# Quad 0's keys in two pieces: a third as floats over SyncE with a cast on ScalarE, and the packed queries in two transfers

## The chip, the cores and the metric

The kernel runs on one core of a Trainium2 chip. The metric is the device time of one execution in microseconds (us), as the median of several runs. A measurement of this kernel tells a difference from no change at about 0.2%, which is 0.49 us here.

## The reference

Eight batches of eight heads attend twice, and a two-layer block with a squared ReLU follows. The first attention has 32 packed queries `p` per head over 576 keys and values; the second has the 576 queries `q` over the 32 packed rows that the first one made.

```python
def _attn_ref(q, k, v, p):                     # q, k, v: 8 x 8 x 576 x 64, p: 8 x 8 x 32 x 64
    def sm_attn(qq, kk, vv):
        s = scale * np.matmul(qq, kk.transpose(0, 1, 3, 2))
        s = s - np.max(s, axis=-1, keepdims=True)
        a = np.exp(s)
        a = a / (np.sum(a, axis=-1, keepdims=True) + 1e-09)
        return np.matmul(a, vv)
    p_packed = sm_attn(p, k, v)
    return sm_attn(q, p_packed, p_packed)
def _moe_ref(x, w_in, w_out):                  # 4608 x 512, 512 x 2048, 2048 x 512
    h = x @ w_in
    r = np.maximum(h, 0.0)
    return (r * r) @ w_out
```

All inputs and the output are float32 in device memory.

## The kernel before

Heads are taken in quads: four heads of 32 rows fill the 128 partitions, so that each of the eight batches (0 to 7) has two quads, 0 and 1. Matmul operands are bf16; the accumulators in PSUM are float32.

The order of the work is written out by hand in the string `ORDER` (L50). `run` takes it word by word, and each word issues the instructions of one step, so that the order on every engine, and on the queues that DMAs are issued from, is the order of the words. The first letters name the step, and the digits name batch and quad (or batch, half and block). A suffix `:a`, `:v` or `:p` picks ScalarE (ACT), VectorE (DVE) or GpSimd (POOL). The words that matter at the head are these.

- `pf` (`p_first`, L222) loads the packed queries of batches 0 and 1 as floats into a part of `gT` that is not yet in use (`p_f`). It issues three DMAs from SyncE (SP), at L225, L268 and L270. A quad whose rows are turned needs two transfers, which `load_rows` makes (L268, L270).
- `P0` and `P1` (`p_cast`, L231 and L235) scale and cast the packed queries of batch 0 and of batch 1 on DVE and turn them there in 32x32 blocks.
- `Lk00`, `Lk01`, `Lv00`, `Lv01` (`load1`) load keys and values of quads 0 and 1 of batch 0. `LA0` and `LB0` load the queries, `Wi..` and `Wo.` the weights. All of these are issued by POOL and cast from float32 to bf16 on the way, and they go through one queue in this order.
- `kT00`, `kT01` (`st_k`, L351) transpose the keys of a quad on DVE, 128x576 pairs each.
- `Z18.0`, `Z2.0`, `Z7.0` and so on (`busy`, L335) are matmuls on zeros, 128x512 each, that keep PE busy; their number is fixed in the word. They start after a memset of the zeros (L187).
- `s100`, `s101` (L375) are the 24 score matmuls of a quad, `m100`, `m101` (L401) the row maxima on DVE, `x100`, `x101` (L413) the exponentials on ACT, and `eT..` (L433), `eo..` (L421) the transposes of the result on PE and their copies to SBUF.

After the first attention of batch 0 come `pv0`, `pp0` (the packed rows), then the second attention in two parts (`A` with 256 columns, `B` with 320), and from about 21 us on the words of the two-layer block: `h` (first layer, L590), `r` (ReLU, L595 or L597), `q` (square, L635 or L633) and `o` (second layer, L648). They are mixed with the attention of the next batch.

The order begins so (L51):

```
pf Lk00 Lk01 Lv00 Lv01 I P0 LA0 P1 Wi00 kT00 Wi10 LB0 Z18.0 s100 Wi01 kT01 Wi11 m100 Z2.0 s101 x100 m101 Wi21 x101 Z7.0
```

Of the kernel before, what the change touches and what calls it, by code (L numbers as in the profile page):

```python
# [9 lines left out]
ALU = mybir.AluOpType  # L10
# [11 lines left out]
D = 64  # L22
# [12 lines left out]

WIDE = range(2, 8)
# [14 lines left out]
pf Lk00 Lk01 Lv00 Lv01 I P0 LA0 P1 Wi00 kT00 Wi10 LB0 Z18.0 s100 Wi01 kT01 Wi11 m100 Z2.0 s101 x100 m101 Wi21 x101 Z7.0  # L51
eT00 eo00:v Z1.0 eT01 rd0 eo01:v Wi20 Z2.0 pv0 pp0 qA01 Lk10 Z2.0 pt0 bd0 qA00 po0:a Z2.1 zA0 Lk11 tA00 tA01 mA01 mA00
sA01:v xA01 sA00:v uA01 xA00 qB00 Wo0 qB01 aA01:p uA00 Z18.1 zB0 wa00 Lv11 tB00 tB01 aA00:p Wa00:a mB00 Z2.1 wa01 mB01
sB00:p Wa01:a TA01 Z1.1 wb01 TA00 Lv10 wb00 xB00 sB01:v h0.0.8 h0.0.9 Wb01:a Wb00:v h0.0.1 h0.0.0 xB01 uB00 r0.0.8:a
r0.0.1:a h0.0.2 uB01 r0.0.9:a aB00:p r0.0.0:a h0.0.3 r0.0.2:v q0.0.4:a h0.0.11 Wo2 aB01:v h0.0.10 q0.0.0:a TB00 TB01
r0.0.3:a r0.0.10:v r0.0.11:a h0.1.0 h0.1.1 q0.0.1:v q0.0.5:a h0.1.9 r0.1.0:v h0.1.8 r0.1.1:a r0.1.9:v LA1 w100 w101
q0.1.0:v r0.1.8:a h0.1.10 W100:v W101:a h0.1.11 h0.1.3 q0.1.4:p h0.1.2 r0.1.10:a r0.1.3:v r0.1.11:a h0.0.4 kT10 r0.1.2:a
LB1 h0.0.13 r0.0.4:a h0.0.5 q0.1.1:a h0.1.14 r0.0.13:v q0.1.5:p h0.0.14 r0.0.5:v h0.1.13 r0.1.14:a kT11 h0.0.15
r0.0.14:a h0.0.6 q0.0.2:a h0.0.12 Wo1 r0.0.15:v s11 r0.1.13:a r0.0.12:v r0.0.6:a Wo3 h0.1.15 q0.0.7:v q0.0.6:a h0.0.7
r0.1.15:v h0.1.4 r0.0.7:a Lv20 h0.1.6 m110 r0.1.4:a h0.1.5 r0.1.6:a h0.1.7 m111 h0.1.12 q0.0.3:a o2.0 x110 r0.1.5:v o2.1  # L60
r0.1.12:v q0.1.7:p o0.0 x111 o3.0 r0.1.7:a eT10 q0.1.6:a o0.1 Pr q0.1.2:v eT11 q0.1.3:v eo10:a o1.0 rd1 eo11:v o3.1 pv1
o1.1 pp1 o0.2 pt1 o1.2 bd1 po1:a o3.2 qA11 w011 w111 qA10 W011:a o0.3 W111:v o2.2 Lv21 o1.3 qB10 zA1 qB11 w010 o2.3 tA11
W010:a tA10 o3.3 mA11 zB1 mA10 sA11 w110 o0.4 sA10 tB11 W110:a o2.4 tB10 o1.4 mB11 xA11 o0.5 xA10 mB10 o1.5 uA10 o2.5
Lk20 sB11 o0.6 uA11 o0.7 xB11 aA10 o1.6 c0:a aA11 o1.7 sB10 o3.4 TA10 c1:a d0 TA11 o2.6 uB11 xB10 h1.0.1 Lk21 h1.0.6 Px
o2.7 r1.0.1:v d1 r1.0.6:v o3.5 aB11 h1.0.0 c2:a h1.0.2 Pt o3.6 r1.0.0:a TB11 o3.7 r1.0.2:a d2 Lk31 Pu:v q1.0.0:a h1.0.4
h1.0.3 c3:a o4.0 r1.0.3:v r1.0.4:a o5.0 kT20 q1.0.1:a h1.0.7 d3 h1.0.5 uB10 o5.1 r1.0.5:a o4.1 r1.0.7:v q1.0.2:a aB10
h1.0.10 h1.0.8 q1.0.3:v r1.0.10:a o4.2 kT21 Lq2 h1.0.9 r1.0.8:a o5.2 r1.0.9:a h1.0.12 TB10 s12 q1.0.4:v r1.0.12:a
h1.0.14 m120 o5.3 Lv30 r1.0.14:a h1.1.1 m121 h1.1.3 r1.1.1:a o5.4 x120 r1.1.3:v h1.0.11 o4.3 r1.0.11:v x121 h1.1.7 kT31
h1.0.15 eT20 Lq3 q1.0.5:a o4.4 r1.0.15:v eT21 r1.1.7:v q1.0.7:a o5.5 rd2 eo20:v eo21:a h1.0.13 h1.1.2 r1.0.13:v o4.5
r1.1.2:v q1.0.6:a h1.1.6 pv2 r1.1.6:v h1.1.8 pp2 h1.1.0 q1.1.1:a r1.1.8:v Lk30 o5.6 qT21 q1.1.3:a o4.6 h1.1.12 r1.1.0:a  # L70
bd2 pt2 qT20 o4.7 bs2:a Lk40 h1.1.5 po2:v r1.1.12:a o5.7 q1.1.0:v c4:a h1.1.10 r1.1.5:v c5:a s22 d4 r1.1.10:v h1.1.4
o6.0 t221 r1.1.4:a h1.1.9 d5 o7.0 q1.1.2:a t220 h1.1.13 r1.1.9:a o6.1 qT30 r1.1.13:a Lq4 h1.1.11 q1.1.4:a m221 w120 w121
r1.1.11:a o6.2 m220 W121:a h1.1.14 h1.1.15 W120:v Lv31 o6.3 r1.1.14:a q1.1.6:a o7.1 o6.4 sb21:v r1.1.15:a Lv40 o7.2
q1.1.5:a kT30 o7.3 q1.1.7:a o7.4 sb20:v Lk41 x221 o6.5 qT31 o7.5 x220 o6.6 su21 o6.7 o7.6 su20 c6:a o7.7 w020 a221 c7:a
d6 w021 o8.0 W020:a a220 o8.1 d7 o8.2 aT21 W021:a o8.3 aT20 o8.4 Lq5 h2.0.1 h2.0.0 r2.0.1:v o8.5 r2.0.0:a o8.6 q2.0.0
h2.0.2 h2.0.3 r2.0.2:v o9.0 Lk50 o8.7 r2.0.3:v h2.0.5 c8:a s13 q2.0.1 r2.0.5:a h2.0.4 d8 m130 o10.0 r2.0.4:a h2.0.6 kT40
h2.0.7 r2.0.6:a o10.1 r2.0.7:a q2.0.2 h2.0.10 Lk51 x130 m131 o9.1 h2.0.8 r2.0.10:a q2.0.3 o9.2 r2.0.8:a kT41 h2.0.13
x131 eT30 h2.0.9 r2.0.13:v o10.2 eo30:a rd3 r2.0.9:v h2.1.1 eT31 q2.0.4 h2.0.14 r2.1.1:a o10.3 r2.0.14:v eo31:a h2.0.11
Lk61 o9.3 r2.0.11:v o9.4 h2.0.12 h2.1.5 q2.0.5 r2.0.12:a pv3 r2.1.5:v h2.0.15 q2.0.6 h2.1.4 pp3 r2.0.15:a o9.5 r2.1.4:v
# [55 lines left out]
class Kernel:  # L135
# [128 lines left out]
    def load_rows(self, x, s, n=0, engine=None):  # L264
# [558 lines left out]
```

## Time and profile before

| what | value |
|---|---|
| three runs | 243.16, 243.31, 243.33 us, median 243.31 us |
| the profiled execution | 243.35 us, of which the span from the first to the last instruction is 241.5 us |
| granted TensorE clock, mean | 0.999 |
| PE busy | 235.4 us (97% of the span) |
| DVE busy | 203.0 us (84%) |
| ACT busy | 142.0 us (59%) |
| POOL busy | 74.8 us (31%) |
| DMA queue of POOL (q0) | 18.55 MB, 54.2% of 16 engines |
| DMA queue of SP (q1) | 9.51 MB, 14.8% of 16 engines |

The profiled execution stands within 0.04 us of the median, so that differences worked out inside it can be set against the runs. Outside the span lie 1.85 us. The page's 40 slices show PE at nine tenths or more nearly everywhere, with the zeros counted as work.

### The profile page before, as it was taken

How to read it: one execution, taken by the hardware profiler on the slowest of the kernel's cores; microseconds unless marked ns; L12 is line 12 of the kernel's file. 1: busy time of each engine (PE TensorE's matmuls, PEld its weight loads, DVE VectorE, ACT ScalarE, POOL GpSimd, SP SyncE). 2: the span in 40 equal slices, each digit the busy share in tenths (PEclk: the TensorE clock that was granted, in tenths of full speed). 3: DMA queues.
4: the chain of work that ended last, by engine and by line, in shares of the span. 5: the costliest groups of instructions: out<-in, count | busy, mean ns of one | idle time of the engine just before them, and what ended most of it. 6: DMA issues, size and time to landing. Idle time of an engine off the chain costs nothing.

```text
span 241.5 us, 6098 instructions
## 1 busy us (share of the span) xinstructions
PE 235.4 (97%) x2415; PEld 125.9 (52%) x2415; DVE 203.0 (84%) x459; ACT 142.0 (59%) x308; POOL 74.8 (31%) x123
## 2 busy tenths in 40 slices
PE   8998899999999999999999999999999999999994
PEld 3544564456544564456555554465545644555542
DVE  2679986999998889989998889997899879987740
ACT  2216993697897557955693647774495346733300
POOL 8637783594585262044303340002000000000000
PEclk9999999999999999999999999999999999999999
DMA  6999999999999979259932974217113111111224
GB/s 103 189 199 210 202 206 206 181 209 210 194 169 212 236 103 136 51 71 209 107 86 28 206 107 66 62 34 105 37 24 76 46 46 43 43 46 43 50 61 109
DMA packets 33404, 28.51 MB, mean 118 GB/s; under 512 B 8160, under 2 KB 28384, under 8 KB 33376
## 3 DMA queue, kind: packets, MB, share of 16 engines
q0 software_dynamic: 26848, 18.55, 54.2%
q1 hardware_dynamic: 6384, 9.51, 14.8%
q8 instruction: 19, 0.31, 0.5%
q14 instruction: 9, 0.07, 0.1%
q10 hardware_dynamic: 144, 0.07, 0.1%
HBM read 37.22 MB, written 9.44 MB: 193 GB/s over the span
## 4 chain that ended last, share of the span: by engine, by line
PE 91%; DMA 4%; ACT 2%; DVE 1%; SPq 0%; issue 0%; POOL 0%; POOLq 0%
PE ps_o L648 50%; PE ps_h L590 26%; PE ps_wp L574 4%; PE ps_idle L335 3%; PE ps_s L375 3%; DMA k_b<-in_k_dram 2%; PE ps_e1T L433 2%; PE ps_pv L457 1%; DMA out_dram<-o_sb 1%; ACT r L595 1%; ACT wp L419 1%; SPq L679 0%; PE ps_ppT L496 0%; ACT gT L633 0%; DVE kT L351 0%
## 5 line engine op out<-in xcount | busy, mean ns | idle before, releaser
L648 PE MATMUL ps_o<-w_out_bf,gT 128*128 128x512 bf16 (+1 forms) x576 | 147.3, 378 | 0.0
L590 PE MATMUL ps_h<-a2T,wp 128*128 128x288 bf16 (+2 forms) x512 | 89.9, 286 | 1.3 <-DVE rs L543 0.6
L595 ACT ACTIVATE r<-ps_h 128x288 bf16<-128x288 f32 (+2 forms) x159 | 61.0, 415 | 47.2 <-PE ps_h L590 42.5
L648 PEld LDWEIGHTS <-gT 128*128 128x128 bf16 x576 | 54.4, 98 | 43.1 <-issue 3.4
L590 PEld LDWEIGHTS <-wp 128*128 128x128 bf16 x512 | 47.7, 98 | 42.4 <-issue 8.0
L597 DVE TENSOR_SCALAR r<-ps_h 128x288 bf16<-128x288 f32 (+2 forms) x97 | 41.9, 447 | 11.1 <-PE ps_h L590 10.5
L635 DVE TENSOR_TENSOR gT<-r 128x576 bf16<-128x576 bf16 (+2 forms) x104 | 45.1, 446 | 2.8 <-ACT r L595 1.8
L419 ACT CAST wp<-ps_wp 128x1024 bf16<-128x1024 f32 (+1 forms) x29 | 27.7, 974 | 9.0 <-PE ps_wp L574 8.9
L419 ACT COPY o_sb<-ps_o 128x512 f32<-128x512 f32 x26 | 15.2, 589 | 12.3 <-PE ps_o L648 10.1
L268 POOL DMA_DIRECT2D k_b<-in_k_dram x28 | 15.2, 544 | 16.5 <-DVE kT L351 7.3
L268 POOL DMA_DIRECT2D q_b<-in_q_dram x16 | 11.0, 690 | 28.8 <-DVE qT L363 25.4
L313 POOL DMA_DIRECT2D v_b<-in_v_dram x12 | 9.4, 779 | 31.5 <-PE ps_pv L457 30.5
L335 PE MATMUL ps_idle<-gT 128*128 128x512 bf16 (+1 forms) x59 | 16.1, 417 | 1.2 <-DVE gT L187 1.2
L413 ACT ACTIVATE e<-ps_s,nm 128x576 bf16<-128x576 f32 x16 | 11.8, 742 | 7.5 <-DVE nm L401 7.4
L633 ACT ACTIVATE gT<-r 128x512 bf16<-128x512 bf16 (+1 forms) x21 | 14.0, 690 | 0.5 <-DVE r L597 0.3
L535 ACT ACTIVATE e<-d 128x576 f32<-128x576 f32 (+2 forms) x20 | 11.7, 599 | 4.1 <-DVE d L529 3.9
L351 DVE STREAM_TRANSPOSE kT<-k_b 128x576 uint32<-128x576 uint32 x16 | 12.3, 767 | 0.6 <-DMA k_b<-in_k_dram 0.6
L363 DVE STREAM_TRANSPOSE qT<-q_b 128x576 uint32<-128x576 uint32 (+2 forms) x20 | 12.4, 633 | 0.0
L541 DVE TENSOR_REDUCE sums<-e 128x18 f32<-128x576 f32 (+2 forms) x20 | 12.2, 608 | 0.1
L401 DVE TENSOR_REDUCE nm<-ps_s 128x1 f32<-128x576 f32 x16 | 11.5, 739 | 0.8 <-PE ps_s L375 0.7
L523 DVE TENSOR_REDUCE mx<-s 128x18 f32<-128x576 f32 (+2 forms) x20 | 11.6, 609 | 0.0
L529 DVE TENSOR_TENSOR d<-s,mx 128x576 f32<-128x576 f32 (+2 forms) x19 | 11.6, 631 | 0.0
(60 smaller groups left out, 179.3 us busy)
## 6 DMA issues: line engine op xcount, KB each, us to landing
out_dram<-o_sb SPq DMA_DIRECT2D x65, 128.0 KB, 2.9
v_b<-in_v_dram POOLq DMA_DIRECT2D x12, 256.0 KB, 5.5
w_out_bf<-in_moe_w_out_dram POOLq DMA_DIRECT2D x4, 512.0 KB, 12.4
q_b<-in_q_dram POOLq DMA_DIRECT2D x6, 288.0 KB, 5.3
q_b<-in_q_dram POOLq DMA_DIRECT2D x12, 144.0 KB, 5.7
k_b<-in_k_dram POOLq DMA_DIRECT2D x12, 108.0 KB, 4.1
gT<-in_v_dram POOLq DMA_DIRECT2D x4, 288.0 KB, 9.7
w_in_bf<-in_moe_w_in_dram POOLq DMA_DIRECT2D x4, 256.0 KB, 9.8
```

Of the source, the lines that this page charges most:

```text
L268: engine.dma_start(x[n:], s[:P - n])
L335: self.nc.tensor.matmul(ps[:, :m], lhsT=self.nought[:, :P], rhs=self.nought[:, :m], start=True, stop=True)
L351: self.nc.vector.transpose(t["kT"][:].rearrange("p s e -> p (s e)").bitcast(U32), t["k"][:].rearrange("p t d -> p (t d)").bitcast(U32))
L363: self.nc.vector.transpose(out.bitcast(U32), x.bitcast(U32))
L419: engine.copy(out, x)
L541: nc.vector.reduce_sum(out=sums[:, x], in_=t["e2"][:, x], axis=AX.X)
L590: self.nc.tensor.matmul(ps, lhsT=t["wp"][:, fb // n, fb % n * P:(fb % n + 1) * P], rhs=t["a2T"][:, s0:s1], start=(qd == 0), stop=(qd == se ...
L595: engine.activation(r, ps, ACT.Relu)
L597: engine.tensor_scalar_max(r, ps, 0.0)
L633: engine.activation(out, r, ACT.Square)
L635: engine.tensor_tensor(out=out, in0=r, in1=r, op=ALU.mult)
L648: self.nc.tensor.matmul(self.o[tt][:, e], lhsT=self.gT[:, fb, a:a + P], rhs=self.w_out_bf[:, fb, e], start=(i == 0), stop=(i == self.NFB - 1))
```

## The change

Quad 0 of batch 0 gets its keys in two pieces. The first third of each row's keys (six of 18, 128x384 floats) is loaded without a cast, by SP, into the last block of `gT`, which is unused then (`Kf0`). ACT casts it into the bf16 tile of the keys (`Kc0:a`). The other two thirds (128x768) come as before, through POOL's queue (`Lh00`). The transpose `kT00` becomes two: `kA00` for the first third and `kB00` for the rest.

The packed queries come in two transfers instead of one: those of batch 0 are issued by ACT (`pf0`), those of batch 1 by SP behind `Kf0` (`pf1`, three DMAs). The word `P1` moves from before `kT00` to behind `m101`.

The words of `ORDER` that differ, with those beside them:

```diff
-pf Lk00 Lk01 Lv00 Lv01 I P0 LA0 P1 Wi00 kT00 Wi10 LB0 Z18.0 s100 Wi01 kT01 Wi11 m100 Z2.0 s101 x100 m101 Wi21 x101 Z7.0
+Kf0 pf0 pf1 Lh00 Lk01 Lv00 Lv01 I P0 LA0 Kc0:a Wi00 kA00 kB00 Wi10 LB0 Z18.0 s100 Wi01 kT01 Wi11 m100 Z2.0 s101 x100 m101 P1 Wi21 x101 Z7.0
```

The rest of `ORDER` is the same. The functions behind these words:

```diff
+FIRST = (slice(0, T // 3), slice(T // 3, T))
...
+        self.k_f = self.gT[:, self.NFB - 1, :].bitcast(F32).rearrange("p (t d) -> p t d", d=D)
...
-    def p_first(self):
+    def p_first(self, b):
 
-        n, qd = 2 * self.NQ, self.NQ - 1
-        self.nc.sync.dma_start(self.p_f[:, :n - 1, :], self.packed(0, n - 1))
-        self.load_rows(self.p_f[:, n - 1, :], self.p[1, qd * QH:].rearrange("h i d -> (h i) d"), qd, self.nc.sync)
+        n, qd, engine = b * self.NQ, self.NQ - 1, self.nc.sync if b else self.nc.scalar
+        if b == 0:
+            engine.dma_start(self.p_f[:, :self.NQ, :], self.packed(0, self.NQ))
+            return
+        engine.dma_start(self.p_f[:, n:n + qd, :], self.packed(n, n + qd))
+        self.load_rows(self.p_f[:, n + qd, :], self.p[b, qd * QH:].rearrange("h i d -> (h i) d"), qd, engine)
...
+    def k_first(self, hf):
+
+        y = FIRST[hf]
+        s = self.k[0, :QH].rearrange("h (l t) d -> (h l) t d", t=T)
+        self.nc.sync.dma_start(self.k_f[:, y, :], s[:, y, :])
+
+    def k_cast(self, engine, hf):
+
+        y = FIRST[hf]
+        t = self.att.setdefault((0, 0), {})
+        self.copy(engine, self.new(t, self.ld, "k", [P, T, D], BF16, "k_b")[:, y, :], self.k_f[:, y, :])
...
     def load1(self, b, qd, n):
...
-        x = t[n] = self.ld.tile([P, T, D], BF16, name="k_b")
+        x = self.new(t, self.ld, "k", [P, T, D], BF16, "k_b")
         s = s.rearrange("h (l t) d -> (h l) t d", t=T)
-        if b in WIDE:
+        if n == "h":
+            self.load_rows(x[:, FIRST[1], :], s[:, FIRST[1], :])
+        elif b in WIDE:
...
-    def st_k(self, t):
+    def st_k(self, t, hf=None):
 
-        t["kT"] = self.tp.tile([P, S, 2], BF16, name="kT")
-        self.nc.vector.transpose(t["kT"][:].rearrange("p s e -> p (s e)").bitcast(U32),
-                                 t["k"][:].rearrange("p t d -> p (t d)").bitcast(U32))
+        y = slice(0, T) if hf is None else FIRST[hf]
+        out = self.new(t, self.tp, "kT", [P, S, 2], BF16)[:, y.start * NP:y.stop * NP]
+        self.nc.vector.transpose(out.rearrange("p s e -> p (s e)").bitcast(U32),
+                                 t["k"][:, y, :].rearrange("p t d -> p (t d)").bitcast(U32))
```

The diff also adds functions for steps such as `st_qP`, `st_z` and `step_f`, and words for them; no word of `ORDER` calls these. On the engines the change comes to this: SP issues four DMAs at the head instead of three, ACT issues one DMA and does one cast ahead of `x100`, POOL issues the same number of DMAs with the first one a third smaller, DVE does three key transposes instead of two, and PE's instructions are the same in number and order.

More of the change, by code (lines that the diff above doesn't have):

```diff
@@ L50 @@
 ORDER = """
-pf Lk00 Lk01 Lv00 Lv01 I P0 LA0 P1 Wi00 kT00 Wi10 LB0 Z18.0 s100 Wi01 kT01 Wi11 m100 Z2.0 s101 x100 m101 Wi21 x101 Z7.0
[L52 to L55, printed above, removed]
@@ L131 @@
-o34.2 o34.3 o33.7 o34.4 c33:v o34.5 o34.6 o34.7 d33 o35.0 c34:v o35.1 o35.2 d34 o35.3 o35.4 o35.5 o35.6 o35.7 c35 d35
+Kf0 pf0 pf1 Lh00 Lk01 Lv00 Lv01 I P0 LA0 Kc0:a Wi00 kA00 kB00 Wi10 LB0 Z18.0 s100 Wi01 kT01 Wi11 m100 Z2.0 s101 x100
+m101 P1 Wi21 x101 Z7.0 eT00 eo00:v Z1.0 eT01 rd0 eo01:v Wi20 Z2.0 pv0 pp0 qA01 Lk10 Z2.0 pt0 bd0 qA00 po0:a Z2.1 zA0
+Lk11 tA00 tA01 mA01 mA00 sA01:v xA01 sA00:v uA01 xA00 qB00 Wo0 qB01 aA01:p uA00 Z18.1 zB0 wa00 Lv11 tB00 tB01 aA00:p
+Wa00:a mB00 Z2.1 wa01 mB01 sB00:p Wa01:a TA01 Z1.1 wb01 TA00 Lv10 wb00 xB00 sB01:v h0.0.8 h0.0.9 Wb01:a Wb00:v h0.0.1
@@ L288, in load1 @@
     def load1(self, b, qd, n):
[L289 removed]
+        s = (self.v if n == "v" else self.k)[b, qd * QH:(qd + 1) * QH]
         t = self.att.setdefault((b, qd), {})
@@ new lines, in st_qP, with st_qE @@
+    def st_qP(self, t, qd, hf):
+        n = self.span(hf)
+        x = self.q_part(t["q"], n)[:, qd]
+        m = (n.stop - n.start) // 2
+        ps = t["ps_q", hf] = self.bank16(0, "ps_q")[:, :m * P].rearrange("p (u c) -> p u c", c=P)
+        for u in range(m):
+            self.nc.tensor.transpose(ps[:, u, :], x[:, 2 * u:2 * u + 2, :].rearrange("p t d -> p (t d)"), self.ident)
+    def st_qE(self, t, engine, hf):
+        n = self.span(hf)
+        y = self.new(t, self.tp, "qT", [P, T // 2, P], BF16)
+        self.copy(engine, y[:, n.start // 2:n.stop // 2, :], t["ps_q", hf])
@@ new lines, in st_z @@
+    def st_z(self, hf):
+        n = self.span(hf)
+        m = (n.stop - n.start) // 2
+        ps = self.turn32("ps_z")[:, :, :self.NQ * m * NP].rearrange("p e (q u i) -> p e q u i", q=self.NQ, i=NP)
+        self.att[0, 0]["ps_z", hf] = ps
+        for u in range(m):
+            for qd in range(self.NQ):
+                t = self.att[0, qd]
+                for h in range(QH):
+                    g = NP * self.group(qd, h)
+                    for e in range(2):
+                        r = slice(D * e, D * e + D)
+                        self.nc.tensor.matmul(ps[g:g + NP, e, qd, u, :],
+                                              lhsT=t["qT"][r, n.start // 2 + u, NP * h:NP * h + NP],
+                                              rhs=t["ppT"][r, NP * h:NP * h + NP], start=True, stop=True)
@@ L354, in st_q, with st_za2 @@
+    def st_za2(self, engine, hf, qd):
+        t, n = self.att[0, qd], self.span(hf)
+        e2, rs = self.z_work(hf)[:, :, qd], self.z_small("rsz", hf)[:, :, qd]
+        a2 = self.new(t, self.tp, "a2", [P, T // 2, NP, 2], BF16)
+        engine.tensor_tensor(out=a2[:, n.start // 2:n.stop // 2].rearrange("p u i e -> p e u i"), in0=e2,
+                             in1=rs.unsqueeze(3).to_broadcast(list(e2.shape)), op=ALU.mult)
     def st_q(self, b, t, qd, hf=None):
@@ L743, in step @@
             make_identity(self.nc, self.ident)
-        elif word == "pf":
-            self.p_first()
+        elif word[:2] == "pf":
+            self.p_first(int(word[2]))
+        elif word[:2] == "Kf":
+            self.k_first(int(word[2]))
+        elif word[:2] == "Kc":
+            self.k_cast(engine, int(word[2]))
         elif word in ("Pr", "Px", "Pt", "Pu"):
```

200 lines of the change are left out of this document (122 added, 78 removed).

## The prediction

> **What bounds the kernel now.** I read the page first, then the chain of waits, the timeline of PE and DVE up to 12.5 us, and the windows of the first microseconds. On the page the chain that ended last is PE nearly throughout:
>
> ```profile
> PE 91%; DMA 4%; ACT 2%; DVE 1%; SPq 0%; issue 0%; POOL 0%; POOLq 0%
> ```
>
> The change touches only the first 11 us, so what counts is which wait starts PE's work there. The chain of waits in order of time (start, length, what) begins:
>
> ```profile
> 1.94 5.80 DMA k_b<-in_k_dram
> 7.74 0.02 issue
> 7.76 0.79 DVE kT L351
> 8.55 0.04 issue
> 8.59 0.69 PE ps_s L375 x24
> 9.28 1.62 PE ps_idle L335 x7
> ```
>
> The keys of quad 1 land at 7.74 us, DVE transposes them, and the scores `s101` start at 8.59. From there the chain stays on PE, on idle matmuls for the most part, and nothing behind waits for a DMA on the path. So the keys of quad 1, not those of quad 0, head the chain. The timeline of DVE shows why quad 0 isn't at stake:
>
> ```profile
> 5.99 0.23 DVE L231 TENSOR_SCALAR p_b<-gT 128x128 bf16<-128x128 f32 x1 [2.48 <-DMA gT<-in_p_dram]
> 6.25 0.24 DVE L235 STREAM_TRANSPOSE pT<-p_b 128x64 uint32<-128x64 uint32 x1
> 6.42 0.73 DVE L351 STREAM_TRANSPOSE kT<-k_b 128x576 uint32<-128x576 uint32 x1
> 7.76 0.78 DVE L351 STREAM_TRANSPOSE kT<-k_b 128x576 uint32<-128x576 uint32 x1 [0.60 <-DMA k_b<-in_k_dram]
> 8.46 1.62 DVE L401 TENSOR_REDUCE nm<-ps_s 128x1 f32<-128x576 f32 x2
> ```
>
> Quad 0's keys land at 6.05 (the first k transfer: issued at 1.25, 4.8 to landing). `P1` runs from 5.99 to 6.50, and `kT00` ends at 7.16. But PE, in its own timeline, isn't free before then:
>
> ```profile
> 4.58 2.79 PE L335 MATMUL ps_idle<-gT 128*128 128x512 bf16 x10
> 7.31 0.69 PE L375 MATMUL ps_s<-kT,pT 32*32 32x192 bf16 x24
> 7.93 0.61 PE L335 MATMUL ps_idle<-gT 128*128 128x512 bf16 x2
> 8.59 0.69 PE L375 MATMUL ps_s<-kT,pT 32*32 32x192 bf16 x24
> 9.22 1.68 PE L335 MATMUL ps_idle<-gT 128*128 128x512 bf16 x7
> ```
>
> The single records say it more finely. The last matmul of `Z18.0` starts at 7.00, the first of `s100` at 7.31, 0.31 later, with no idle time between. `kT00` had ended 0.15 before; after the transpose of quad 1 a matmul follows its end by 0.05. So `s100` was held by the idle block, by about 0.1 us. The last matmul of `Z2.0` starts at 8.16; with the same 0.31 `s101` could start at 8.47. It starts at 8.59, held by `kT01` (ends 8.54, plus 0.05). PE therefore waited for the keys for 8.59 - 8.47 = 0.12 us, and no more.
>
> **The keys' landing.** POOL's queue moves 128x384 fewer bf16 elements ahead of quad 1's keys: 98 KB. The windows (per engine busy time and count, then granted clock, DMA share, GB/s) show how fast the queue is and what is free before:
>
> ```profile
> 1.00:2.00 1.00, 0.81 (x2) 0.28 (x3) 0.55 (x4) 1.00 (x1) 0.75 (x2) 1.00 0.07 17
> 2.00:3.00 1.00, 1.00 (x4) 0.43 (x3) 0.01 (x1) 0.02 (x1) 1.00 (x2) 1.00 0.71 114
> 4.00:5.00 1.00, 1.00 (x3) 0.30 (x2) 0.00 (x0) 0.00 (x0) 0.93 (x3) 1.00 1.09 195
> 5.00:6.00 1.00, 1.00 (x5) 0.48 (x4) 0.01 (x1) 0.00 (x0) 1.00 (x3) 1.00 1.05 189
> ```
>
> At 182 GB/s (mean of 4 to 8 us: 195, 189, 164, 181) 98 KB take 0.54 us. By packets it is less: in the records of 4 to 6 us a packet of 2304 bytes takes about 0.185 us, one of 768 bytes later about 0.08; a packet of 1536 bytes is then near 0.13, eight per DMA engine, 0.42 us. The other way, the 197 KB of floats have to move somewhere. SP's first transfer moves its first packets at 1.86, POOL's queue at 2.66; in the second window only 0.07 and in the third 0.71 of the DMA engines were busy, so that the floats go mostly into room that was empty. Bounds for the landing of quad 1's keys: nothing gained (7.74) to 0.54 earlier (7.20). I take 7.3, near the packets' figure, since only the floats' tail meets POOL's packets.
>
> Beside the row on the share, the Trainium skill (DMA: Bandwidth & Descriptors, section Issuing engines are not separate DMA queues) speaks against the change: DMAs from several engines run on the same 16 DMA engines and interleave, and only issue time is saved. By it the landing stays at 7.74 and the time at 243.35. The trace agrees that the queues share from 4 us on (share at or above 1), not that there is nothing to gain before.
>
> **The sum.** With the landing at 7.3, `kT01` runs from 7.32 to 8.10. `s101` needs PE at 8.47 at the earliest, and any landing up to 7.61 allows that (7.61 + 0.02 + 0.78 + 0.05). So `s101` goes from 8.59 to 8.47: **-0.12 us**. The maxima follow: `m100` can start at 8.02 instead of 8.46, but `m101` waits for the end of `s101`. `x101` then goes from 10.12 to 9.99. `Z7.0` and `eT00` run on PE without a wait (9.22 to 11.24 before), all 0.12 earlier. Whatever `x100` gains (0.43) ends in `Z7.0`.
>
> **What is added.** *Cast on ACT:* not in the trace; bounds from the copy of 128x256 out of PSUM (0.37) and the exponential of 128x320 (0.47), a little above the latter, 0.53. ACT stands idle for 7.2 us before `x100`, so it costs nothing on the path; if it came late it would hold `kA00`, `kB00` and `kT01` behind it on DVE. The float third should land near 3.3: the first p transfer on SP took 2.2 us from issue at 0.74, plus some for twice the bytes. ACT's own DMA issue (0.46 by SP's row) and table load (1.28) end near 2.5, ahead of that. *`kA00`, `kB00`:* 0.73 in two parts with some 0.05 more, on DVE from about 3.9 and from 5.6, in the gap from 3.51 to 5.99. *`P1`:* 0.23 + 0.25 between `m101` (ends 9.96) and `eo00` (11.15), where DVE was idle for 1.19; its p, issued last on SP, took at most 4.1 from issue before and has until 10. Its absence ahead of `kT00` gives nothing, since `Z18.0` is later. *Queues:* POOL's DMA waits end earlier by up to the landing's gain; the queries land at 12.04 and are needed at 13.21, values at 10.64 and needed at 12.2, `w_in` at 18.03 and needed at 19.0, so earlier landings only add slack. SP's issues behind are outputs from 40 us on. Each of these: 0.
>
> Sum: 243.35 - 0.12 = 243.23, or 243.19 from the median. I say **243.2**.
>
> **Rivals.**
> *The whole gain of the landing shows.* The page's chain taken at its word: the DMA heads it, so its 0.44 comes out whole. That needs `Z18.0` to end earlier, by two of its matmuls switching from 0.427 to 0.216 each. The Trainium skill (TensorE: Matmul & The Clock Gate, section What's actually happening) has the switch moving by 500 ns between runs. For it: ten of the 18 ran at 0.427, then eight at 0.216, so the switch sets the end. Against it: three runs within 0.17 us, and a later switch would have shown in them. `s101` would start at 7.3 + 0.85 = 8.15: 243.35 - 0.44 = 242.9; with the landing at 7.2 it is 242.8, beyond 0.2%.
> *No gain.* The floats slow POOL's first packets as much as the smaller transfer saves; 243.35. For it: the third p transfer of SP took 4.1 against 2.2, so the queues did collide. Against it: the empty second window.
> *Slower.* The float third lands late, and everything in DVE's fixed order behind `kA00` waits. From its landing L: cast 0.53, `kA00` 0.30, `kB00` 0.50, `kT01` 0.78, four handovers of 0.05 make 2.3; `s101` is later than before from L = 6.3, and loses 0.49 from L = 6.8. At 4.1 from issue, the slowest p, L = 4.84, harmless; at 7.1, the median of the first two v transfers, L = 7.84 and `s101` starts at 10.1, +1.5: 244.9. For it: SP's small packets did wait behind POOL's. Against it: `Kf0` is issued first and starts before POOL's queue does.
>
> **How the numbers follow.** Forecast (a gain of 0.05 to 0.3): 0.55. Whole gain or more: 0.19, of which 0.14 beyond 0.49. No gain to a few tenths lost: 0.14. Late floats: 0.12, nearly all beyond 0.49. Faster 0.14, same 0.73, slower 0.13. The range reaches from the whole gain with the landing at its bound, 242.8, to 243.7, a landing of the floats near 6.7.
>
> **What would show it.** After: keys of quad 1 landing between 7.2 and 7.6; `s100` at 7.31 still, `s101` near 8.47 right behind `Z2.0` with no gap; `P1` at 10.0 and no wait ahead of `eo00`; the chain of waits beginning on PE idle matmuls in place of the DMA. It would be wrong if `s100` itself moved, if `kT01` still ended behind `Z2.0`, or if ACT's cast started later than 5 us.

## The result, and the profile after

The changed kernel takes 244.31 us (median of 18 runs, 243.51 to 245.79) against 243.31 for the kernel before in the same session (18 runs): a ratio of 1.0037, 95% interval 1.0023 to 1.0051. That is 1.0 us slower where -0.12 was forecast, and beyond the range. The profiled execution took 244.56 us, its span 242.7.

The page's chain of waits has changed hands at its beginning. PE's share is down from 91% to 87%, and POOL, with 0% before, has 3%:

```profile
PE 87%; DMA 4%; POOL 3%; ACT 2%; issue 2%; POOLq 0%; ACTq 0%
```

The chain in order of time (start, length, what) no longer runs through the keys and PE's idle matmuls, but through POOL's own instructions:

```profile
5.10 0.69 POOL w_in_bf L263
5.79 10.21 DMA w_in_bf<-in_moe_w_in_dram
...
16.27 0.49 POOL k_b L277
16.77 2.06 issue
...
18.84 0.77 POOL w_out_bf L268
19.61 0.01 issue
19.63 0.44 POOL a L637
```

What holds POOL for those 2.06 us stands in its timeline (start, length, what, in brackets the idle time before it and what ended that):

```profile
18.84 0.78 POOL L268 DMA_DIRECT2D w_out_bf<-in_moe_w_out_dram  x1 [2.07 <-DMA q_b<-in_q_dram]
19.63 0.63 POOL L637 TENSOR_TENSOR a<-e,rs 128x256 bf16<-128x256 f32 x1
20.19 0.73 POOL L329 DMA_DIRECT2D gT<-in_v_dram  x1
20.93 0.63 POOL L637 TENSOR_TENSOR a<-e,rs 128x256 bf16<-128x256 f32 x1
```

The issue of `Wo0` waits until the queries' second part (`LB0`) has landed, at 18.55 (17.02 before), and the products of the second attention queue behind it on POOL. Before, the same issue stood at 17.30, with the same wait, and the products at 18.09 and 19.39:

```profile
17.30 0.78 POOL L261 DMA_DIRECT2D w_out_bf<-in_moe_w_out_dram  x1 [1.92 <-DMA q_b<-in_q_dram]
```

Earlier, the timelines of ACT, DVE and PE show the changed head itself:

```profile
3.40 0.51 ACT L507 CAST k_b<-gT 128x384 bf16<-128x384 f32 x1 [0.86 <-DMA gT<-in_k_dram]
```

```profile
4.10 0.34 DVE L373 STREAM_TRANSPOSE kT<-k_b 128x192 uint32<-128x192 uint32 x1
5.71 0.58 DVE L373 STREAM_TRANSPOSE kT<-k_b 128x384 uint32<-128x384 uint32 x1 [1.28 <-DMA k_b<-in_k_dram]
8.55 0.78 DVE L373 STREAM_TRANSPOSE kT<-k_b 128x576 uint32<-128x576 uint32 x1 [2.26 <-DMA k_b<-in_k_dram]
...
10.79 0.22 DVE L238 TENSOR_SCALAR p_b<-gT 128x128 bf16<-128x128 f32 x1
```

```profile
1.19 6.80 PE L356 MATMUL ps_idle<-gT 128*128 128x512 bf16 x18 [1.19 <-DVE gT L191]
7.92 0.69 PE L463 MATMUL ps_s<-kT,pT 32*32 32x192 bf16 x24
8.54 0.60 PE L356 MATMUL ps_idle<-gT 128*128 128x512 bf16 x2
9.38 0.69 PE L463 MATMUL ps_s<-kT,pT 32*32 32x192 bf16 x24 [0.23 <-DVE kT L373]
```

The floats were on time (landed 3.38, cast from 3.40). But quad 1's keys landed at 8.53, not at 7.74 as before, and `s101` started at 9.38, 0.79 later than before and 0.23 behind a free PE. The windows (the stretch's length and PE's busy time first, the granted clock, DMA share and GB/s of all queues last) show when less was moved:

```profile
2.00:3.00 1.00, 1.00 (x4) 0.43 (x3) 0.00 (x0) 0.54 (x1) 1.00 (x2) 1.00 0.90 235
4.00:5.00 1.00, 1.00 (x3) 0.30 (x2) 0.43 (x2) 0.00 (x0) 0.93 (x3) 1.00 1.00 151
5.00:6.00 1.00, 1.00 (x4) 0.44 (x3) 0.29 (x1) 0.00 (x0) 1.00 (x3) 1.00 1.13 144
```

The floats did go into the third microsecond (235 GB/s against 114). From 4 to 6 us, when they are done, the DMA engines are as busy as before (1.00 and 1.13 against 1.09 and 1.05) and move nearly a quarter less: 151 and 144 GB/s against 195 and 189.

The records of single packets say where in the transfer the time was lost. Of the last 128 packets of 2304 bytes (quad 1's keys), half had ended by 5.98 (6.02 before), nine tenths by 7.24 (6.70) and the last by 8.22 (7.40). So the first half kept its time, and the tail was late. Nine of the packets that start between 4 and 6 us take more than 0.4 us, against two before.

**Two bounds.** The fifth `h` word of the order (`h0.0.2`, two matmuls) starts on PE at 22.90 before and at 23.91 after. The recorded expectations call its start the fifth layer-1 matmul, and "the matmul" below is its first one. PE's rows that begin with it, before and after:

```profile
22.90 1.20 PE L590 MATMUL ps_h<-a2T,wp 128*128 128x256 bf16 x8 [0.58 <-DVE rs L543]
```

```profile
23.91 1.20 PE L678 MATMUL ps_h<-a2T,wp 128*128 128x256 bf16 x8 [0.68 <-ACT r L683]
```

What ended the wait just before it stands in brackets; the ways below lead to it from further back. Everything behind it up to the last PE instruction (237.79 and 238.81) is shifted as a whole. The spans differ by 0.2 more, behind that instruction; this end of the span was 3.67 us before and 3.88 after, and 3.5 to 4.2 over all profiles. Two ways lead to the matmul. One starts with `s101`, on PE through the idle blocks and the second attention: 14.31 us. The other starts with the landing that POOL's issue of `Wo0` waits for: 5.36 us to that matmul by way of POOL's products. The later one decides: before 8.59 + 14.31 = 22.90 against 17.02 + 5.36 = 22.38; after 9.38 + 14.31 = 23.69 against 18.55 + 5.36 = 23.91. In the other profiles below the later one gives the start within 0.05 too, where both ways exist and where `Wo0` no longer stands ahead of the products and only the first is left; the one exception is told there (batch 1's p late).

### The profile page after: what moved, and what is told of

Read it like the earlier page. It is cut to its first block, busy times and chain, and to the rows that moved or that the text cites. A ratio compares the mean times of both kernels' runs of the same rounds, so it can differ in the third digit from the quotient of the medians.

```text
span 242.7 us, 6104 instructions
## 1 busy us (share of the span) xinstructions
PE 236.1 (97%) x2415; PEld 126.2 (52%) x2415; DVE 203.4 (84%) x460; ACT 142.5 (59%) x309; POOL 74.7 (31%) x123
## 4 chain that ended last, share of the span: by engine, by line
PE 87%; DMA 4%; POOL 3%; ACT 2%; issue 2%; POOLq 0%; ACTq 0%
PE ps_o L742 52%; PE ps_h L678 26%; DMA w_in_bf<-in_moe_w_in_dram 4%; PE ps_wp L662 4%; PE ps_s L463 3%; PE ps_e1T L521 2%; PE ps_pv L545 1%; ACT r L683 1%; POOL gT L329 1%; ACT wp L507 1%; POOL k_b L275 1%; POOL a L637 0%; ACT gT L727 0%; PE ps_o L747 0%; PE ps_ppT L584 0%
## 5 line engine op out<-in xcount | busy, mean ns | idle before, releaser
L356 PE MATMUL ps_idle<-gT 128*128 128x512 bf16 (+1 forms) x59 | 16.8, 429 | 1.2 <-DVE gT L191 1.2
L373 DVE STREAM_TRANSPOSE kT<-k_b 128x576 uint32<-128x576 uint32 (+2 forms) x17 | 12.4, 732 | 3.6 <-DMA k_b<-in_k_dram 3.5
```

Of the source, the lines that this page charges most:

```text
L356: self.nc.tensor.matmul(ps[:, :m], lhsT=self.nought[:, :P], rhs=self.nought[:, :m], start=True, stop=True)
L373: self.nc.vector.transpose(out.rearrange("p s e -> p (s e)").bitcast(U32), t["k"][:, y, :].rearrange("p t d -> p (t d)").bitcast(U32))
```

## The experiments

Theory: the loss comes from the floats over SyncE, which make the transfers behind them on POOL's queue land later, and from what waits for those (the two bounds). Rivals: ScalarE's queue, p's pieces, the smaller transfer on POOL's queue, the moved `P1`, or PE's idle block `Z18.0`, whose end moves from one execution to the next. "Before" is the kernel before on the same chip, 243.26 to 243.43 us throughout. The ratios are not the quotients of the two medians and differ from these by up to 0.0012. The landings and starts are each from one profiled execution. Diffs of the order show only the words that differ and their neighbours.

### Each part alone

Float third, cast and two key transposes, with p in one go on SyncE behind it (the word `pf9`):

```diff
-Kf0 pf0 pf1 Lh00
+Kf0 pf9 Lh00
```

> The keys' part of the change alone: the float third over SP, its cast on ACT and the two key transposes, with the packed queries as before in one go on SP behind the float third (three DMAs: 96, 24 and 8 KB), and P1 behind the maxima. In the changed kernel's profile quad 1's keys landed at 8.53 us instead of 7.74 and the queries' second part at 18.55 instead of 17.02. Theory K (the float third in SP's queue costs POOL's queue more than the smaller transfer saves): this one is as slow as the changed kernel, near 244.2, with quad 1's keys landing past 8.2. Theory Q (the packed queries on two rings, small packets beside POOL's keys, cost it): this one is at 243.2, keys at 7.3 to 7.5. Theory C (only the clock's switch came late in that profile): no difference from before beyond 0.2.

p alone (ScalarE and SyncE), keys whole:

```diff
-Kf0 pf0 pf1 Lh00 ... Kc0:a Wi00 kA00 kB00
+pf0 pf1 Lk00 ... Wi00 kT00
```

> The other part alone: the keys of quad 0 in one transfer over POOL and one transpose as before; the packed queries of batch 0 issued by ACT, those of batch 1 by SP, P1 behind the maxima. Theory K: as before, 243.3, quad 1's keys landing near 7.7. Theory Q: near 244.2, keys past 8.2. Theory C: as before.

Only `P1` moved, in the kernel before:

```diff
-LA0 P1 Wi00 kT00 ... m101 Wi21
+LA0 Wi00 kT00 ... m101 P1 Wi21
```

> Only the word P1 is moved behind m101; everything else is the kernel before. By the prediction the move costs and gains nothing, since kT00 is held by nothing but PE's idle block: 243.3, landings as before. Rival: what runs on DVE beside the landings, or P1 between the maxima and the copies, costs some tenths: 243.6 or more, with a wait ahead of eo00.

| part | median | ratio to before, 95% |
|---|---|---|
| float third (and `P1`) | 243.79 | 1.0017 (1.0007 to 1.0027) |
| p over ScalarE and SyncE (and `P1`) | 243.51 | 1.0004 (0.9995 to 1.0013) |
| `P1` alone | 242.87 | 0.9979 (0.9969 to 0.9990) |

The first two hold the moved `P1` too. The first lies between its forecasts (243.2 and 244.2), and the gain of the third was not forecast. Against the third, the float third costs 0.92 us and p's two queues 0.64. With the 0.46 that `P1` gains they give 243.33 - 0.46 + 0.92 + 0.64 = 244.43 for the whole change; 244.31 was measured. By the medians the change is a good move with two bad ones on top. The 0.92 rests on the times alone: the one profile of the float third (243.47, of its lower times) had quad 1's keys at 7.69, no later than before, and `LB0` at 16.44.

### POOL's products, and p's pieces

The change, with `Wo0` and `Lv11` behind POOL's products:

```diff
-qB00 Wo0 qB01 aA01:p ... wa00 Lv11 tB00 ... sB00:p Wa01:a
+qB00 qB01 aA01:p ... wa00 tB00 ... sB00:p Wo0 Lv11 Wa01:a
```

> The changed kernel with the DMA issues Wo0 and Lv11 moved behind POOL's two products of the A part and its subtraction. In the changed kernel's profile POOL waited with Wo0 until 18.82 for the queries' landing, and the products stood behind it: PE's delay grew there from 0.79 to 1.01 us. Theory P (the wait on POOL is a second loss): 0.2 to 0.3 us less than the changed kernel, about 244.0. Rival (the head's delay is the whole loss, or the queries' transposes on DVE wait for the same landing): no gain, 244.2 to 244.3.

244.09 us, 1.0027 (1.0010 to 1.0043). The bound through POOL is gone, but quad 1's keys landed at 8.68 and `s101` started at 9.53: 9.53 + 14.31 = 23.84, and the matmul started at 23.84. With both bounds late, taking one away brought 0.07 in the profiles (23.91 to 23.84) and 0.22 in the medians, where the intervals overlap.

The change, with batch 1's p issued only after the key transposes (`pf8`, into the key tile, which is free by then) and cast behind `eo01`:

```diff
-Kf0 pf0 pf1 Lh00 ... kB00 Wi10 ... m101 P1 Wi21 ... eo01:v
+Kf0 pf0 Lh00 ... kB00 pf8 Wi10 ... m101 Wi21 ... eo01:v P1
```

> The changed kernel with batch 1's packed queries issued only when quad 0's key transposes are done (near 7 us instead of 1.2 to 2.6; SP waits for DVE) and cast behind the copy eo01. What it takes out of the head are three small transfers on SP's queue (64 KB in 256-byte packets) beside POOL's keys. Theory Q' (these packets beside the keys cost the queue: in the changed kernel's profile POOL's queue had moved 273 KB by 5.5 us against 341 before): quad 1's keys land before 8.0, 243.4 to 243.7. Theory K (the floats of the keys cost it by themselves): keys past 8.2, 244.1 to 244.3 as the changed kernel.

244.39 us, 1.0039 (1.0022 to 1.0057); keys of quad 1 at 8.70. The small pieces of batch 1's p aren't the cause.

The same on whole keys, with batch 0's p issued by SyncE (`pf7`):

```diff
-pf Lk00 ... LA0 P1 Wi00 kT00 Wi10 ... eo01:v
+pf7 Lk00 ... LA0 Wi00 kT00 pf8 Wi10 ... eo01:v P1
```

> The same for the kernel before: keys whole over POOL, the packed queries of batch 0 alone on SP at the head, those of batch 1 issued behind kT00 and cast behind eo01. Theory Q': still faster than the run with only P1 moved (242.87), 242.4 to 242.7, quad 1's keys landing before 7.5. Theory K: as that run, 242.9.

244.26 us, 1.0039 (1.0025 to 1.0053), but for a reason of its own: batch 1's p landed at 13.07, `P1` waited for it and held `pp0` behind it on DVE. For the landing it says what was wanted: with only 66 KB of p at the head the keys landed at 5.52 and 6.97.

### Where P1 stands, and the idle block

`P1` between the two key transposes, then `P1` behind the maxima with three idle matmuls fewer:

```diff
-LA0 P1 Wi00 kT00 Wi10
+LA0 Wi00 kT00 P1 Wi10
```

> The kernel before with P1 between kT00 and kT01 on DVE, in place of ahead of kT00. Moving P1 behind the maxima gave 0.46 us (interval 0.24 to 0.75) where I had forecast nothing. Theory D1 (P1 held back kT00 and by it s100, in runs where PE's idle block ends early): this one gains the same, near 242.9. Theory D2 (the last p transfer often lands late, and P1 then holds back kT01): this one stays near 243.3, P1 having still to be done before kT01.

```diff
-LA0 P1 Wi00 kT00 Wi10 LB0 Z18.0 ... m101 Wi21
+LA0 Wi00 kT00 Wi10 LB0 Z15.0 ... m101 P1 Wi21
```

> The kernel before with P1 behind m101, and the idle block at the head three matmuls shorter (Z15.0 instead of Z18.0), so that PE is free for s100 0.65 us sooner (three at 0.216). My prediction had PE's idle block hold s101 at 8.47 once the keys come earlier. Theory Z (the block bounds the head in most runs): 242.5 or less, s100 near 7.1 as soon as its keys are transposed. Rival (the keys' landing bounds it, the block is cover): 242.9, as with Z18.0, with idle time of PE ahead of s101; or slower, if the clock's switch comes later by it.

243.11 us, 0.9999 (0.9986 to 1.0012), and 243.10 us, 0.9988 (0.9973 to 1.0004). In the first, `s101` was 0.43 earlier than before (8.16), and the gain was lost whole: the queries' second part landed at 17.53, 17.53 + 5.36 = 22.89, and the matmul started at 22.89. The second bound lies so near behind the first that an earlier head alone need not pay. In the second, the shorter block left PE no earlier: 13 of its 15 matmuls took 0.427, and `s100` started at 7.35 (7.31 before). It holds the moved `P1` as well, and its interval shows neither the gain of 0.46 nor its absence.

### What in the head delays POOL's queue

The change with all transfers of the head on SyncE, floats first, then p first:

```diff
-        n, qd, engine = b * self.NQ, self.NQ - 1, self.nc.sync if b else self.nc.scalar
+        n, qd, engine = b * self.NQ, self.NQ - 1, self.nc.sync
```

> The changed kernel, with the first p transfer issued by SyncE behind the float third, so that ScalarE issues no DMA at the head. Theory A (two queues of floats at the head, SyncE's and ScalarE's, hold up POOL's queue together): quad 1's keys land at 7.4 to 7.8 again, the queries' second part at 16.5 to 17.5, s101 starts at 8.4 to 8.8, time 243.2 to 243.7. Theory B (the float third or the smaller transfer of quad 0's keys alone does it): quad 1's keys land past 8.2, the queries' second part at 18 or later, the fifth layer-1 matmul past 23.6, time 244.0 to 244.5.

```diff
-Kf0 pf0 pf1 Lh00
+pf0 Kf0 pf1 Lh00
```

> As the run before it, with the order of the first two transfers on SyncE turned round: p first, then the float third. Theory A: as there, keys of quad 1 at 7.4 to 7.8, 243.2 to 243.7; the float third lands some 0.4 later than 3.4, still ahead of its cast's need. Theory B: keys of quad 1 past 8.2 and 244.0 to 244.5, in both orders alike.

244.02 us, 1.0025 (1.0012 to 1.0037), and 243.81 us, 1.0025 (1.0003 to 1.0046); keys of quad 1 at 8.15 and 7.96. That is between the two theories, which these runs don't decide.

Whole keys, p as in the change, and the float third loaded though nothing uses it; then the same with floats from other rows of memory:

```diff
-pf0 pf1 Lk00
+Kf0 pf0 pf1 Lk00
```

> The kernel with p alone changed (ScalarE's and SyncE's transfers, keys whole over POOL, batch 1's p behind the maxima), and the float third of quad 0's keys loaded over SyncE as well, into a place where nothing uses it. Theory A (SyncE's floats beside ScalarE's p hold up POOL's queue): quad 1's keys land at 8.4 or later, the queries' second part past 17.9, 244.1 to 244.6. Theory C (the reshaped transfer of 1536-byte packets on POOL's queue does it): quad 1's keys land at 7.6 to 8.0, as with p alone changed, 243.4 to 243.7.

```diff
-        s = self.k[0, :QH].rearrange("h (l t) d -> (h l) t d", t=T)
+        s = self.k[7, QH:].rearrange("h (l t) d -> (h l) t d", t=T)
```

> The kernel with whole keys and an unused float third, with one word changed: the floats are read from the last keys in memory (batch 7, quad 1), not from the rows that POOL's first transfer reads at the same time. If two queues reading the same rows of memory hold each other up, quad 1's keys land at 7.6 to 8.0 again and the time is 243.4 to 243.7. If it is the floats' traffic as such, they land past 8.3 and the time is 244.0 to 244.5.

244.32 us, 1.0045 (1.0028 to 1.0062), and 244.54 us, 1.0047 (1.0031 to 1.0064). The chain of the first begins

```profile
1.93 6.68 DMA k_b<-in_k_dram
8.61 0.02 issue
8.63 0.79 DVE kT L373
```

so the keys land at 8.61, against 7.80 without the floats; in the second at 8.75. It is the floats' transfer itself, here beside p on two queues: not the reshaped transfer on POOL's queue (here the keys are whole), not the cast (there is none), not two queues reading the same rows. Nor is it PE's idle block: in the first, `s100` started at 7.20, earlier than before, and `s101` at 9.47. The time of the first is that of the change (244.31), whose keys landed at 8.53, so that the 98 KB less on POOL's queue bought 0.08 in the landing and nothing in the time. The queries' second part is not late in each of these profiles: it landed at 17.10 in the first (17.02 before) and at 18.77 in the second.

### Both bounds moved

Keys whole, batch 1's p late and cast in a gap of DVE behind `zA0`, `LB0` ahead of `Wi10`, three idle matmuls fewer:

```diff
-pf Lk00 ... LA0 P1 Wi00 kT00 Wi10 LB0 Z18.0 ... zA0
+pf7 Lk00 ... LA0 Wi00 kT00 pf8 LB0 Wi10 Z15.0 ... zA0 P1
```

> Keys whole, as before; only batch 0's p at the head on SyncE, batch 1's p issued behind the first key transpose and cast behind zA0, in a gap of VectorE at 14.1 to 14.6; the queries' second part issued ahead of the second part of w_in; three idle matmuls fewer ahead of the first scores. Two bounds were read from the nine profiles: the fifth layer-1 matmul starts at the later of s101 plus 14.31 and the landing of the queries' second part plus 5.36. If that holds, both are moved here: s101 at 8.1 to 8.5, the queries' second part near 15.7 (a bound at 21.1, off), the fifth layer-1 matmul at 22.4 to 22.8 against 22.90, time 242.6 to 243.0. Rival: w_in, now second, lands late in its place (needed from 19.0), or the bound through s101 has another wait behind it: 243.2 to 243.6, no gain.

243.28 us, 0.9998 (0.9987 to 1.0010): a miss, and the trace says why. `s101` started at 7.78, 0.81 earlier than before, but the issue of `Wo0` now waited for `w_in`'s second part, which had changed places with `LB0` and landed at 17.25: POOL's issues use eight semaphores in turn, and each waits for the landing of the eighth transfer before it, whatever that is. 17.25 + 5.36 = 22.61; measured 22.60.

So the next kernels take `Wo0` and `Lv11` from ahead of the products as well: with the float third (p and floats on SyncE), without it, and the kernel before with order changes alone.

```diff
-Kf0 pf0 pf1 Lh00 ... kB00 Wi10 LB0 Z18.0 ... m101 P1 Wi21 ... zA0 ... Wo0 qB01 aA01:p ... Lv11 tB00 ... sB00:p
+pf7 Kf0 Lh00 ... kB00 pf8 LB0 Wi10 Z15.0 ... m101 Wi21 ... zA0 P1 ... qB01 aA01:p ... tB00 ... sB00:p Wo0 Lv11
```

> The float third and its cast as in the change, but p of batch 0 first on SyncE, no transfer on ScalarE's queue, p of batch 1 issued behind the key transposes, the queries' second part ahead of w_in's, w_out and the values of batch 1 issued behind POOL's products, three idle matmuls fewer. If ScalarE's queue beside SyncE's is what holds POOL's queue up: quad 1's keys at 7.0 to 7.6, s101 at 7.9 to 8.5, 242.5 to 243.1, level with the next kernel. If the floats cost by themselves: keys at 7.8 to 8.3, s101 at 8.7 to 9.2, the fifth layer-1 matmul 14.31 behind it at 23.0 to 23.5, 243.4 to 243.9.

```diff
-pf7 Kf0 Lh00 Lk01 ... Kc0:a Wi00 kA00 kB00 pf8
+pf7 Lk00 Lk01 ... Wi00 kT00 pf8
```

> The same without the float third: the kernel with p late and the queries early, with w_out's first part and batch 1's values issued behind POOL's products. There the fifth layer-1 matmul was held at 22.60 through POOL, 5.36 behind the landing (17.25) of w_in's second part, which had become the transfer that w_out's issue waits for, while s101 at 7.79 would have let it start at 22.10. If the two bounds are right, it starts at 14.31 behind s101, at 21.9 to 22.3, and the time is 242.3 to 242.8. Rival: POOL's products wait for something else, or the late w_out and values bring a wait behind: 243.1 to 243.5.

```diff
-LA0 P1 Wi00 kT00 Wi10 LB0 Z18.0 ... m101 Wi21 ... Wo0 qB01 aA01:p ... Lv11 tB00 ... sB00:p
+LA0 Wi00 kT00 Wi10 LB0 Z15.0 ... m101 P1 Wi21 ... qB01 aA01:p ... tB00 ... sB00:p Wo0 Lv11
```

> The kernel before with nothing but its order changed: batch 1's p cast behind the maxima, three idle matmuls fewer, w_out's first part and batch 1's values issued behind POOL's products. By the two bounds: keys of quad 1 at 7.1 to 7.8 as in the kernels with this head, the fifth layer-1 matmul 14.31 behind s101 at 22.3 to 23.0, 242.6 to 243.2, since the second bound no longer takes back an early head. Rival (the second bound never mattered here): as with the casts moved and fifteen idle matmuls, 243.0 to 243.2.

| kernel | median | ratio, 95% | quad 1's keys | `s101` + 14.31 | matmul started |
|---|---|---|---|---|---|
| with the float third | 243.45 | 1.0009 (0.9992 to 1.0026) | 8.55 | 23.71 | 23.71 |
| without it | 243.29 | 0.9991 (0.9981 to 1.0000) | 6.98 | 22.26 | 22.25 |
| order alone | 242.98 | 0.9981 (0.9972 to 0.9989) | 7.05 | 22.21 | 22.26 |

The order alone beats the kernel before by its interval (0.3 to 0.7 us); so did `P1` alone, and the two can't be told apart. The kernel without the float third is a miss: its matmul started 0.65 earlier than before, 242.3 to 242.8 was forecast, and its time is level with the kernel before. Of the 0.65, 0.49 were left at the last PE instruction (237.30), and the end of the span behind that was 0.28 longer (3.95 against 3.67). The windows of 4 to 6 us show once more what the floats do, first with them, then without:

```profile
4.00:5.00 1.00, 1.00 (x3) 0.29 (x2) 0.38 (x1) 0.33 (x1) 0.93 (x3) 1.00 1.05 144
5.00:6.00 1.00, 1.00 (x4) 0.43 (x3) 0.48 (x1) 0.00 (x0) 1.00 (x3) 1.00 0.98 145
```

```profile
4.00:5.00 1.00, 1.00 (x3) 0.29 (x2) 0.00 (x0) 0.00 (x0) 0.93 (x3) 1.00 1.06 196
5.00:6.00 1.00, 1.00 (x4) 0.39 (x3) 0.45 (x1) 0.00 (x0) 1.00 (x3) 1.00 1.07 198
```

The profile and the median of the kernel with floats must not be mixed: its twelve times lie in two groups, seven from 242.77 to 243.56 and five from 244.07 to 244.60, and the profiled execution (244.34) is of the upper. It seems that in this kernel the late landing comes in some executions and not in others; only the profiled one shows its landing. It shows the late landing with SyncE's queue alone, without ScalarE's. The changed kernel's own 18 times spread too (six from 243.51 to 243.89), and its profile is of the upper ones.

With the order alone the fifth `h` word starts 0.64 earlier than before (22.26 against 22.90), the ninth only 0.34 (24.11 against 24.45). That is a cost of the moved issues. `Lv11` now stands with `Lv10` ahead of POOL's product of 128x320: the two issues hold POOL until 22.70, and the product starts at 22.71, though the reciprocal that it waits for ended at 22.21 (before, it started 0.14 behind that, at 22.99). So it runs beside DVE's product,

```profile
21.35 1.35 POOL L308 DMA_DIRECT2D gT<-in_v_dram  x2
22.71 0.74 POOL L549 TENSOR_TENSOR a<-e,rs 128x320 bf16<-128x320 f32 x1
```

```profile
21.99 0.22 DVE L543 RECIPROCAL rs<-sums 128x10 f32<-128x10 f32 x1
...
23.02 0.81 DVE L549 TENSOR_TENSOR a<-e,rs 128x320 bf16<-128x320 f32 x1
```

and DVE's takes 0.81, where before it took 0.51, started 0.06 before the end of POOL's:

```profile
23.66 0.51 DVE L549 TENSOR_TENSOR a<-e,rs 128x320 bf16<-128x320 f32 x1
```

That is 0.3 on the chain there, and the other three kernels with these issues moved have 0.81 or 0.82 as well. DVE's ends at 23.83, 0.38 behind the end of POOL's (23.45); before it ended 0.45 behind it. The Trainium skill (SBUF — State Buffer, section SBUF: two separate sides) has such an operation with two inputs from SBUF blocked by one on POOL for as long as that runs; these rows agree with it in the main, though a product that only starts at 23.45 and takes its 0.51 would end at 23.96. At the last PE instruction 0.58 are left (237.21 against 237.79), in the medians 0.36.

### ScalarE's queue

In the last kernels with and without the float third, batch 0's p issued by ScalarE:

```diff
-            self.nc.sync.dma_start(self.p_f[:, :self.NQ, :], self.packed(0, self.NQ))
+            self.nc.scalar.dma_start(self.p_f[:, :self.NQ, :], self.packed(0, self.NQ))
```

> The kernel with the float third in the repaired order, with one word changed: batch 0's p is issued by ScalarE instead of SyncE. By the medians so far, p over ScalarE (and in two transfers) cost 0.64 us over p by SyncE with whole keys (243.51 against 242.87), and the float third 0.92 (243.79 against 242.87). If ScalarE's issue itself costs, this is 0.4 to 0.8 above its twin (243.45): 243.9 to 244.3. If it was the splitting of p in two, or chance, it is level with the twin: 243.3 to 243.6.

> The same word changed in the kernel with whole keys, p late and both bounds moved (243.29 with p by SyncE). If ScalarE's issue itself costs: 243.7 to 244.1, with quad 1's keys 0.3 or more behind 6.95. If not: 243.1 to 243.5, with the keys at 6.9 to 7.1. The difference between this run and the one before it prices the float third once more: 0.4 to 0.9 expected.

With the floats 244.04 us, 1.0038 (1.0017 to 1.0058): 0.59 above its twin, though the intervals just overlap. Without them 243.13 us, 0.9993 (0.9982 to 1.0003): 0.16 below its twin. So ScalarE's queue shows no cost by itself. That two hardware queues at once cost something fits both the pair with the floats and p alone above, but the intervals don't settle it. The float third costs 0.91 here (244.04 - 243.13), as in the parts alone (0.92), and only 0.16 between the twins with p by SyncE (243.45 - 243.29); that difference stays open.

Over all twenty profiles the landing of quad 1's keys goes with what the hardware queues carry at the head: 6.93 to 6.98 with 66 KB of p (four profiles), 7.05 to 7.80 with 131 KB (six, the kernel before among them), 7.69 to 8.75 with the floats (ten, the change among them).

## Why the prediction was wrong

**The landing is the step that failed.** "Bounds for the landing of quad 1's keys: nothing gained (7.74) to 0.54 earlier (7.20). I take 7.3". It was 8.53. A bound on the late side was missing, on the grounds that the floats go "mostly into room that was empty". They did go there, and in the two microseconds after them all queues together still moved nearly a quarter less, and the tail of quad 1's keys came late. An unused float third on whole keys cost 0.81 in the landing (8.61 against 7.80), more than the 0.42 to 0.54 that the smaller transfer was to save. That saving itself was 0.08 between the two profiles (8.61 to 8.53). The rule of the Trainium skill that was held against the change (DMA: Bandwidth & Descriptors, section Issuing engines are not separate DMA queues) had the right sign: a second issuing engine brought no room. By it the landing stayed at 7.74 and the time at 243.35; the runs went beyond that.

**"earlier landings only add slack"** looked at the queues in one direction only, and not at the queries' second part at all. It landed 1.53 later, POOL waited for it with `Wo0`, and that became the last bound, by 0.22. In the rows before the wait stood there, ended by `q_b` at 17.30, with 0.52 of slack (22.90 - 22.38). How far the floats make this landing late is open: it was at 17.10 with the unused floats and at 16.44 with the float third alone.

**"Its absence ahead of `kT00` gives nothing, since `Z18.0` is later"**: `P1` alone gained 0.46 (interval 0.24 to 0.75). The one profile of that kernel is of its slowest time (243.42) and doesn't show where, so the place of the gain stays open. `Z18.0` is no fixed wall: 8 to 13 of its matmuls ran at 0.427, and `s100` behind it started between 6.91 and 7.94 in the profiles with eighteen. The prediction took "three runs within 0.17 us" for a sign that the switch stays; eighteen runs of the same kernel spread over 1.39 (242.90 to 244.29). The Trainium skill (TensorE: Matmul & The Clock Gate, section What's actually happening) gives the switch a play of 500 ns to either side; the 1.03 us between these starts agrees with that. In the profiled execution after, thirteen ran at 0.427, so `s100` was 0.61 later, within what the other kernels show, and even with keys in time `s101` could have started at 9.08 at best (7.92 plus the 1.16 from 7.31 to 8.47 that the prediction worked out). So in that profile 0.49 of the 0.79 by which `s101` was late is the idle block's, and 0.30 the keys'.

**The rivals.** "Slower" had the right side with the wrong mechanism: late floats holding DVE. The floats landed at 3.38 (forecast near 3.3), the cast took 0.51 (forecast 0.53), the two transposes 0.34 and 0.58 (forecast 0.73 and some more), and `P1` ran at 10.79 without a wait. "No gain", with POOL's first packets slowed as much as the transfer saves, was nearest in mechanism and stopped at zero.

**What would have told.** The text named it: "if `s100` itself moved, if `kT01` still ended behind `Z2.0`". Both came.

Not settled: why POOL's queue has this late tail after the floats are through. The records show some of its packets of 2304 bytes between 4 and 6 us taking 0.6 to 1.3 us where 0.19 is usual; they don't tell which DMA engine or which part of the memory path held them.

## What to carry to other kernels

A transfer put into an empty stretch of the DMA engines isn't free for the queue that starts behind it: give the landing of that queue a late bound too, of the added bytes' time (197 KB at 182 GB/s would be 1.1 us; 0.79 and 0.81 were lost here). Before an early wait is worked on, look for the second wait just behind it: here a DMA issue on POOL that waits for the landing of an earlier transfer and has POOL's arithmetic queued behind it. Moving such an issue behind the arithmetic frees that arithmetic and can hold up the next: here a product of 128x320 was held until 22.71 and ran into DVE's. And where a change has several parts, the one that looked like housekeeping may be the one that pays (`P1`, 0.24 to 0.75).

## What the runs showed of the hardware

- 197 KB of floats on SyncE's queue, landed by 3.8 us, go with 90 to 177 GB/s in the two windows from 4 to 6 us in seven profiles (the change among them), against 168 to 210 in the ten without floats. In the three kernels with floats and all of p on SyncE's queue at the head (keys at 7.69, 7.96 and 8.15) the two windows' mean was 182 to 200, some of it p's own bytes.
- The late landing is a tail: in the change half of the packets of quad 1's keys had ended by 5.98 (6.02 before) and the last by 8.22 (7.40).
- In these kernels an issue on POOL's queue waits for the landing of the eighth transfer before it: `Wo0` for `LB0` (17.02, issued 17.30), and with two transfers swapped for `w_in` (17.25, issued 17.53).
- A tensor-tensor product of 128x320 on DVE takes 0.81 when it starts 0.43 before the end of one on POOL, and 0.51 when it starts 0.06 before that end.
